# Four interleaved sequence layers on one core: a new order of all the work, and another last chunk

## The chip, the cores and the metric

The kernel runs on one core of one Trainium2 chip. A core has four engines that compute side by side, each with its own instruction queue: TensorE (PE, matrix products), VectorE (DVE), ScalarE (ACT) and GpSimd (POOL). SyncE (SP) issues nearly all DMAs here, in the order in which they stand in its queue. An engine takes its instructions in order: one that waits holds up all that stand behind it. The metric is the device time of one execution in microseconds (us).

## The reference

The input x has 2048 tokens of 640 channels, in bfloat16. Four layers are added to it one after the other, A, B, A, B, each behind a layer norm:

```python
x = A_x
x = x + A(layernorm(x)); x = x + B(layernorm(x), B_k, B_v, ...)
x = x + A(layernorm(x)); x = x + B(layernorm(x), B_k, B_v, ...)
```

Layer A is a diagonal state-space layer with 640 complex states. With `Lam_bar = exp(dt * Lam)` and `B_bar = ((Lam_bar - 1) / Lam) * B` it runs `h = Lam_bar * h + B_bar u_t` over the tokens and gives `2 Re(C h) + Dskip * u`.

Layer B multiplies its input by a long convolution: `k` is convolved with four taps per channel, multiplied by `v`, and the product is convolved along all 2048 tokens with the kernel `ssm_k` by FFT; `kv * ssm_D` is added. Call the result Y. Then `B(q) = q * Y`, with q the layer-normed x. Y does not depend on x, and both B layers use the same one. Both A layers have the same weights.

## The kernel before

**The work.** Y is computed first, in five passes of 128 channels (`y_pass`). A pass has FFT stages named KA, KB (of the kernel), VA, VB (of `k` times `v`), a product in frequency on DVE (pw, L1289 to L1294), and the way back (IB, a DMA transpose tt at L1326, IA, and the store to a scratch tensor `ysd` in DRAM at L1352). A stage is a handful of groups of matmuls, typically 16 of 128 columns (L1208, L1232 to L1237, L1313, L1342), each followed by the eviction of one PSUM tile, either on ACT (L384) or on DVE (L386). There are four PSUM tiles of 1024 columns. Beside the passes run the set-up of A's weights (`a_setup_tasks`: L543, L547, L563, L578, L599) and five blocks that make `k` times `v` (`kv_tasks`, L1163).

**Layer A** goes in four chunks of 512 tokens; a chunk has four quarters of 128 tokens. Per chunk:

- layer norm: statistics (in the first A by `bn_stats` at L698, later sums and squares on ACT at L668 and L673), the root on ACT (L678), its reciprocal on DVE (L683, L685), and its application (id: ACT L718 or DVE L720);
- a DMA transpose (tu, L748);
- the input projection (bp, L762 and L765) in groups of 40, 40 and 20 matmuls of 256 columns, each evicted by ACT at L384;
- three DVE products of 2560 columns (ri, L784 to L786), the carry (L795, L796), two scans (sc, L800, 1290 columns each), the carry for the next chunk (cy, L811 to L813), three more products (ro, L823 to L825);
- the output product in quarters (cp, L851: 30 or 25 matmuls in the second A), each evicted with the residual (xe: L863 on DVE, or ACT L859 in the first A).

Pairs of tokens share one scan step, so a chunk has 256 steps. The first A reloads its x (L1482) instead of keeping it. The scan of a chunk needs the carry of the chunk before, so the scans of one layer are a chain.

**Layer B** per chunk: load of Y from `ysd` (L1500), layer norm as above, its application (u, L718 or L720), one product with Y for the whole chunk (mm, L915, 2560 columns) and four additions (m, L921 in the first B; L923 in the second), and in the second B two stores of two quarters, 320 KB each (L886). In the second B's last chunk each quarter is a group of its own: statistics, u, a product of 640 columns (L915), an addition on DVE or POOL (L923), and a store of 160 KB (L881). Its last quarter takes another form: `(x + nmean) * Y` (L900), which needs only the mean, and then `rstd * that + x` (L904), which needs the root.

**What sets the order.** All of this is written as tasks: `S.add(name, engine, estimate, tasks before it, emit, uses=buffers)`. Before anything is emitted, `Sched.run` plays the tasks through once with their estimated durations. Whenever an engine is free, it takes the ready task of the highest rank, where the rank is minus the task's number in the table `WHEN`; a number is roughly the time at which a task should go, and it is a rank only, so a task never goes before those that it depends on. The order of the starts that come out is the order in which the instructions are emitted, so it is fixed on every engine. A task with two engines, such as `("act", "dve")`, takes the second when the first is busy for longer than the second number of its entry.

```python
t.rank, t.wait = (-when[0], when[1]) if isinstance(when, tuple) else (-when, 0.3)
...
cands = [t for t in ready if eng in t.engs and (t.engs[0] == eng or eng_free[t.engs[0]] > now + t.wait) and can(t)]
...
t = max(cands, key=lambda t: (t.rank, -t.idx))
```

Buffers also shape the order. The large SBUF tiles (13 of one size, 6 of double size) and the four PSUM tiles are handed out as tasks come up, and a task starts only when a tile is free for it.

Of the kernel before, what the change touches and what calls it, by code (L numbers as in the profile page):

```python
# [52 lines left out]
    "warm": -1.35, "yt_io0": 2.41, "yt_ph0": 8.42, "yt_sin0": 10.61, "yt_neg0": 12.73, "yt_io6": 10.07, "yt_ph6": 9.01, "yt_sin6": 12.27, "yt_neg6":  # L53
    15.91, "yt_io12": 13.05, "yt_ph12": 14.25, "yt_sin12": 15.9, "yt_neg12": 18.93, "yt_Ci": 20.28, "yt_Si": 37, "yt_nsi": 49, "yt_f0": 3.06, "yt_f2":
    4.09, "yt_f3": 7.55, "yt_f4": 6.22, "yt_h0": 0.91, "yt_h1": 0.33, "yt_h2": 5.52, "yt_h3": 5.63, "kv_dsl": 2.15, "kv_kd": 2.92, "kv_k0": 10.81,
    "kv_k1": 13.94, "kv_k2": 15.71, "kv_d0": 6.65, "kv_d1": 5.29, "kv_d2": 8.81, "kv_ds0": 11.35, "kv_lk0": 4.2, "kv_lv0": 5.45, "kv_mm0:0": 14.43,
    "kv_ev0:0": 16.51, "kv_mm0:1": 10.83, "kv_ev0:1": 13.08, "kv_st0": 17.9, "kv_ds1": 9.15, "kv_lk1": 12.7, "kv_lv1": 18.64, "kv_mm1:0": 19.27,
    "kv_ev1:0": 21.4, "kv_mm1:1": 21.75, "kv_ev1:1": 23.83, "kv_st1": 35.3, "kv_ds2": 18.43, "kv_lk2": 33, "kv_lv2": 29.5, "kv_mm2:0": 38.59, "kv_ev2:0":
    39.32, "kv_mm2:1": 43.65, "kv_ev2:1": 49.83, "kv_st2": 46.49, "kv_ds3": 43.37, "kv_lk3": 41.7, "kv_lv3": 45.49, "kv_mm3:0": 48.44, "kv_ev3:0": 50.96,
    "kv_mm3:1": 57.37, "kv_ev3:1": 61.07, "kv_st3": 92.99, "kv_ds4": 61.29, "kv_lk4": 49.28, "kv_lv4": 68.94, "kv_mm4:0": 73.9, "kv_ev4:0": 74.18,  # L60
    "kv_mm4:1": 69.76, "kv_ev4:1": 73.84, "kv_st4": 73.7, "a_pl": -0.06, "a_p0": 12.27, "a_p1": 16.9, "a_p2": 17.67, "a_p3": 18.1, "a_p4": 20.22, "a_p5":
    23.7, "a_p6": 27.16, "a_lamd": 27.66, "a_f": 28.77, "a_dd": 19.76, "a_ldB0": 1.15, "a_ldB1": -0.78, "a_wl00:0": 40.5, "a_wl00:1": 28.3, "a_wc00:0":
    44.32, "a_wm00:0": 48.24, "a_wc00:1": 49.59, "a_wm00:1": 52.87, "a_wl01:0": 44, "a_wl01:1": 31.8, "a_wc01:0": 48.88, "a_wm01:0": 52.09, "a_wc01:1":
    54.1, "a_wm01:1": 53.61, "a_wl02:0": 45.16, "a_wl02:1": 45.15, "a_wc02:0": 53.34, "a_wm02:0": 59.85, "a_wc02:1": 61.61, "a_wm02:1": 62.85, "a_wl03:0":
    70.24, "a_wl03:1": 64.21, "a_wc03:0": 77.95, "a_wm03:0": 76.93, "a_wc03:1": 78, "a_wm03:1": 78.68, "a_wl04:0": 66.45, "a_wl04:1": 65.36, "a_wc04:0":
    69.09, "a_wm04:0": 75.62, "a_wc04:1": 78.54, "a_wm04:1": 79.09, "a_b00:0": 10.52, "a_b0e0:0": 9.18, "a_b00:1": 8, "a_b0e0:1": (8.6, 99), "a_b00:2":
    13.66, "a_b0e0:2": (15.32, 0), "a_b00:3": 4.32, "a_b0e0:3": (8.39, 0.8), "a_b00:4": 17.45, "a_b0e0:4": (18.19, 0), "a_b01:0": 6.91, "a_b0e1:0": (7.2,
    0.8), "a_b01:1": 11.61, "a_b0e1:1": (14.74, 1.5), "a_b01:2": 4.71, "a_b0e1:2": (6, -1), "a_b01:3": 5.91, "a_b0e1:3": (6.61, 0), "a_b01:4": 8.47,
    "a_b0e1:4": (11.54, 1.5), "a_b10:0": 43.09, "a_b1e0:0": (45.04, 0.8), "a_b10:1": 40.99, "a_b1e0:1": (41.95, 3), "a_b10:2": 30.58, "a_b1e0:2": 31.69,
    "a_b10:3": 36.64, "a_b1e0:3": (39.19, 1.5), "a_b10:4": 47.48, "a_b1e0:4": (48.2, 3), "a_b11:0": 45.38, "a_b1e1:0": (46.36, 0.8), "a_b11:1": 32.76,  # L70
    "a_b1e1:1": (33.78, 6), "a_b11:2": 41.55, "a_b1e1:2": (40.73, -1), "a_b11:3": 31.52, "a_b1e1:3": 32.67, "a_b11:4": 29.62, "a_b1e1:4": (30.57, 0),
    "a_gm0": 80.21, "a_ge0": (84.11, 99), "a_gm1": 93.26, "a_ge1": 96.39, "a_gm2": 83.55, "a_ge2": (87.02, 6), "a_gm3": 89.92, "a_ge3": (93.2, 99),
    "a_gm4": 97.3, "a_ge4": (100.43, 0.8), "a_wl10:0": 85.18, "a_wl10:1": 91.79, "a_wc10:0": 95.59, "a_wm10:0": 101.44, "a_wc10:1": 122.34, "a_wm10:1":
    124.48, "a_wl11:0": 96.08, "a_wl11:1": 94.88, "a_wc11:0": 99.69, "a_wm11:0": 102.22, "a_wc11:1": 119.01, "a_wm11:1": 120.86, "a_wl12:0": 267.43,
    "a_wl12:1": 125.35, "a_wc12:0": 132.96, "a_wm12:0": 134.36, "a_wc12:1": 136.45, "a_wm12:1": 138.84, "a_wl13:0": 130.78, "a_wl13:1": 128.72,
    "a_wc13:0": 134.01, "a_wm13:0": 137.32, "a_wc13:1": 137.15, "a_wm13:1": 140.24, "a_wl14:0": 147.32, "a_wl14:1": 146.18, "a_wc14:0": 150.74,
    "a_wm14:0": 151.96, "a_wc14:1": 155.43, "a_wm14:1": 157.14, "a_ti": 21.54, "a_ta": 22.3, "a_t0": 24.96, "a_t1": 101.91, "a_t2": 108.08, "yq0_kl":
    8.92, "yq0_ka": 16.35, "yq0_KA:m0": 18.34, "yq0_KA:e0": (19.68, 1.5), "yq0_KA:m1": 21.46, "yq0_KA:e1": (22.64, 0.8), "yq0_KA:m2": 18.74, "yq0_KA:e2":
    (21.48, 6), "yq0_KA:m3": 19.03, "yq0_KA:e3": (20.58, 3), "yq0_KB:m0": 24.22, "yq0_KB:e0": (27.08, 99), "yq0_KB:m1": 24.89, "yq0_KB:e1": (26.18, 0),
    "yq0_KB:m2": 26.78, "yq0_KB:e2": 28.25, "yq0_KB:m3": 27.82, "yq0_KB:e3": (29.15, 6), "yq0_KB:m4": 23.99, "yq0_KB:e4": (27.98, 99), "yq0_vl": 20.98,  # L80
    "yq0_VA:m0": 31.28, "yq0_VA:e0": (31.91, 0.8), "yq0_VA:m1": 29.09, "yq0_VA:e1": (30.05, 3), "yq0_VA:m2": 32.18, "yq0_VA:e2": (32.81, 3), "yq0_VA:m3":
    29.37, "yq0_VA:e3": (30.95, 3), "yq0_VB:m0": 37.52, "yq0_VB:e0": (38.54, 0), "yq0_VB:m1": 34.93, "yq0_VB:e1": (36.27, 99), "yq0_VB:m2": 35.83,
    "yq0_VB:e2": (37.17, 1.5), "yq0_VB:m3": 34.04, "yq0_VB:e3": (35.37, 3), "yq0_VB:m4": 37.29, "yq0_VB:e4": (38.1, -1), "yq1_kl": 25.7, "yq1_ka": 32.42,
    "yq1_KA:m0": 38.31, "yq1_KA:e0": (39.88, -1), "yq1_KA:m1": 33.34, "yq1_KA:e1": (34.37, 6), "yq1_KA:m2": 40.32, "yq1_KA:e2": (40.95, 1.5), "yq1_KA:m3":
    33.62, "yq1_KA:e3": (34.34, -1), "yq1_KB:m0": 45.98, "yq1_KB:e0": (46.97, 0), "yq1_KB:m1": 55.1, "yq1_KB:e1": (56.01, 0), "yq1_KB:m2": 42.17,
    "yq1_KB:e2": (43.42, 0), "yq1_KB:m3": 50.15, "yq1_KB:e3": (51.4, 6), "yq1_KB:m4": 48.22, "yq1_KB:e4": (48.92, 0.8), "yq0_pw": 39.67, "yq0_IB:m0":
    54.21, "yq0_IB:e0": 55.94, "yq0_IB:m1": 52.95, "yq0_IB:e1": (54.57, 99), "yq0_IB:m2": 51.18, "yq0_IB:e2": (52.39, 99), "yq0_IB:m3": 52.09,
    "yq0_IB:e3": (53.31, -1), "yq0_IB:m4": 53.57, "yq0_IB:e4": (56.19, 99), "yq0_tt": 63.03, "yq1_vl": 49.03, "yq1_VA:m0": 54.86, "yq1_VA:e0": 56.03,
    "yq1_VA:m1": 53.39, "yq1_VA:e1": (53.81, 0), "yq1_VA:m2": 56.58, "yq1_VA:e2": (57.29, 0), "yq1_VA:m3": 56.61, "yq1_VA:e3": (51.46, 99), "yq1_VB:m0":
    60.95, "yq1_VB:e0": (65.88, 1.5), "yq1_VB:m1": 61.23, "yq1_VB:e1": (63.37, 0.8), "yq1_VB:m2": 62.8, "yq1_VB:e2": (66.49, 6), "yq1_VB:m3": 57.44,  # L90
    "yq1_VB:e3": (67.16, 0), "yq1_VB:m4": 62.47, "yq1_VB:e4": (62.27, 0), "yq0_IA:m0": 64.58, "yq0_IA:e0": (69.19, 0), "yq0_IA:m1": 66.1, "yq0_IA:e1":
    (67.34, 1.5), "yq0_st": 78.73, "yq2_kl": 48.68, "yq2_ka": 55.97, "yq2_KA:m0": 65.34, "yq2_KA:e0": (47.37, 6), "yq2_KA:m1": 66.58, "yq2_KA:e1": (67.98,
    0), "yq2_KA:m2": 66.35, "yq2_KA:e2": (71.01, 99), "yq2_KA:m3": 64.39, "yq2_KA:e3": (64.57, 0), "yq2_KB:m0": 79.33, "yq2_KB:e0": (81.23, 0),
    "yq2_KB:m1": 58.15, "yq2_KB:e1": (74.22, 0.8), "yq2_KB:m2": 71.59, "yq2_KB:e2": (78.27, 0.8), "yq2_KB:m3": 70.55, "yq2_KB:e3": (73.3, 99),
    "yq2_KB:m4": 77.69, "yq2_KB:e4": (78.01, 99), "yq1_pw": 66.29, "yq1_IB:m0": 73.36, "yq1_IB:e0": (75.43, 0), "yq1_IB:m1": 74.89, "yq1_IB:e1": (77.3,
    99), "yq1_IB:m2": 76.2, "yq1_IB:e2": (77.28, -1), "yq1_IB:m3": 76.99, "yq1_IB:e3": (78.62, 6), "yq1_IB:m4": 76.2, "yq1_IB:e4": (77.89, 1.5), "yq1_tt":
    86.38, "yq2_vl": 76.55, "yq2_VA:m0": 77.71, "yq2_VA:e0": (80.89, 0), "yq2_VA:m1": 79.71, "yq2_VA:e1": (81.79, 3), "yq2_VA:m2": 82.99, "yq2_VA:e2":
# [772 lines left out]
def b_chunk(S, nc, R, small, c, lname, s_x, sums_in, x_ready, s_Y, y_ready, sums_out, out, groups):  # L870
# [3 lines left out]
    def finish(q, t_m):  # L874
        ready.append(t_m)
        if out is None:
            return
# [11 lines left out]
    for qs in groups:  # L889
# [4 lines left out]
        for i, q in enumerate(qs):  # L894
# [11 lines left out]
            else:  # L906
# [6 lines left out]
                def e_mm(_, qs=qs):  # L913
                    b = s_b.get()[:, qs[0]:qs[-1] + 1, :]
                    nc.vector.tensor_tensor(b, b, s_Y.get()[:, qs[0]:qs[-1] + 1, :], ALU.mult)  # L915
# [627 lines left out]
```

## Time and profile before

| | us |
|---|---|
| median of 3 runs (lowest, highest) | 381.21 (380.71, 381.98) |
| the profiled execution itself | 381.21 |
| span of its profile | 379.5 |
| PE busy | 338.3 (89%) |
| DVE busy | 317.2 (84%) |
| ACT busy | 252.1 (66%) |
| POOL busy | 24.0 (6%) |

The span is what the engines' records cover; the 1.71 us between it and the execution's own time lie around it. Busy times are averages over stages with different limits: passes of FFT and set-up until about 140 us, then A and B chunks of the two halves, the last output quarters until 368.7, and what comes after the last matmul. So the profile has to be read by stretches, and a wait counts only where the engine that sets the pace is the one that waits. The granted TensorE clock (PEclk) is given as a share of full speed; its mean was 0.964. Where it is 0.5, a matmul takes twice its time while PE shows as busy. In rows of instructions, `b<-ps` means that a buffer is written from PSUM, `x16` counts instructions, and `<-DVE b L825` after a wait names what ended it.

### The profile page before, as it was taken

To read this page: it belongs to the slowest core of one execution; us is meant where nothing else is said; L and a number is where in the kernel's file an instruction comes from. 1 tells how busy PE (TensorE), PEld (TensorE's weight loads), DVE (VectorE), ACT (ScalarE), POOL (GpSimd) and SP (SyncE) were. 2 spreads that over 40 slices of the span, in tenths; PEclk is the share of its full clock that TensorE was granted. 3 is DMA by queue.
4 is the path that set the end of the run, shared out by engine and by line. 5 is a ranking of instruction groups with operands and counts; after the bars stand their busy time and mean duration, and the time that the engine had idled before them with its cause. 6 is when DMAs were issued, how large, how long until landed. Compare 5 with 4: busy or idle time off the path is not lost. (4 is left out here: it accounts for less than half of the span.)

```text
span 379.5 us, 8447 instructions
## 1 busy us (share of the span) xinstructions
PE 338.3 (89%) x3565; PEld 251.5 (66%) x3565; DVE 317.2 (84%) x474; ACT 252.1 (66%) x400; POOL 24.0 (6%) x54
## 2 busy tenths in 40 slices
PE   8787988889996899999999999979999999994780
PEld 8446867676685779989566766745867756852350
DVE  8689698886998888699999669914999899889586
ACT  2999878896899976864426577288592574910462
POOL 4650030000000000000000000000000000000022
PEclk9899999999998989999999999989999999998796
DMA  8979998899956993771752527005132003213003
GB/s 232 207 170 195 198 212 175 147 250 265 194 105 114 208 167 86 140 156 46 120 133 55 209 71 195 15 0 74 66 67 75 1 2 69 80 73 128 0 19 121
DMA packets 119000, 45.91 MB, mean 121 GB/s; under 512 B 111661, under 2 KB 113458, under 8 KB 118962
## 3 DMA queue, kind: packets, MB, share of 16 engines
q1 hardware_dynamic: 118816, 45.36, 55.3%
q8 instruction: 28, 0.46, 0.5%
q14 instruction: 10, 0.08, 0.1%
q10 hardware_dynamic: 146, 0.01, 0.0%
HBM read 17.38 MB, written 7.86 MB: 67 GB/s over the span
## 5 line engine op out<-in xcount | busy, mean ns | idle before, releaser
L384 ACT ACTIVATE b<-ps 128x1024 bf16<-128x1024 f32 (+3 forms) x121 | 106.2, 946 | 25.7 <-PE ps L765 18.8
L851 PEld LDWEIGHTS <-b 128*128 128x128 bf16 x880 | 68.5, 99 | 61.2 <-DVE b L825 8.0
L851 PE MATMUL ps<-W,b 128*128 128x128 bf16 (+1 forms) x640 | 99.4, 305 | 10.1 <-DVE b L825 7.7
L718 ACT ACTIVATE b<-b,nmr,rstd 128x640 bf16<-128x640 f32 (+1 forms) x46 | 39.7, 911 | 28.0 <-DVE nmr L685 26.6
L762 PE MATMUL ps<-b,BT 128*128 128x256 bf16 x400 | 57.3, 274 | 0.9 <-DMA b<-b 0.6
L765 PE MATMUL ps<-b,BT 128*128 128x256 bf16 x400 | 56.9, 273 | 0.0
L800 DVE TENSOR_TENSOR_SCAN b<-rtab,b 128x1290 bf16<-128x1290 f32 x16 | 44.7, 2832 | 0.2
L762 PEld LDWEIGHTS <-BT 128*128 128x128 bf16 x400 | 38.6, 98 | 5.7 <-issue 1.2
L765 PEld LDWEIGHTS <-BT 128*128 128x128 bf16 x400 | 39.3, 98 | 4.7
L673 ACT ACTIVATE junk<-b,nmean 128x640 bf16<-128x640 f32 x48 | 39.7, 827 | 1.4
L1232 PE MATMUL ps<-b,b 128*128 128x128 bf16 x170 | 35.9, 224 | 4.0 <-ACT b L384 3.9
L386 DVE CAST b<-ps 128x1024 bf16<-128x1024 f32 (+2 forms) x28 | 29.1, 1059 | 11.9 <-PE ps L1237 6.0
L1235 PE MATMUL ps<-b,b 128*128 128x128 bf16 x170 | 36.1, 223 | 0.0
L1237 PE MATMUL ps<-b,b 128*128 128x128 bf16 x150 | 33.6, 224 | 0.0
L1234 PE MATMUL ps<-b,b 128*128 128x128 bf16 x150 | 33.6, 224 | 0.0
L851 PE MATMUL ps<-G,b 128*128 128x512 bf16 (+1 forms) x160 | 27.0, 299 | 0.0
L668 ACT ACTIVATE nmean<-sums 128x4 f32<-128x4 f32 (+1 forms) x15 | 3.0, 202 | 35.5 <-DVE b L863 25.5
L1163 PE MATMUL ps<-b,fd 128*128 128x512 bf16 x80 | 20.3, 397 | 4.5 <-ACT b L384 1.6
L923 POOL TENSOR_TENSOR b<-b,b 128x640 bf16<-128x640 bf16 x3 | 4.8, 1638 | 306.1 <-DMA out_dram<-b 306.1
L859 ACT ACTIVATE b<-ps 128x640 f32<-128x640 f32 x15 | 10.4, 695 | 14.8 <-PE ps L851 14.8
L1313 PE MATMUL ps<-b,b 128*128 128x128 bf16 x160 | 19.1, 219 | 0.9 <-DVE b L386 0.6
L1208 PE MATMUL ps<-FA,b 64*128 64x128 bf16 x320 | 14.8, 223 | 5.1 <-ACT b L384 3.8
(203 smaller groups left out, 591.5 us busy)
## 6 DMA issues: line engine op xcount, KB each, us to landing
b<-in_A_x_dram SPq DMA_DIRECT2D x8, 640.0 KB, 4.6
b<-ysd SPq DMA_DIRECT2D x8, 640.0 KB, 4.2
b<-in_B_ssm_k_dram SPq DMA_DIRECT2D x5, 512.0 KB
kvd<-b SPq DMA_DIRECT2D x5, 512.0 KB, 5.0
b<-kvd SPq DMA_DIRECT2D x5, 512.0 KB, 4.7
ysd<-b SPq DMA_DIRECT2D x5, 512.0 KB, 5.0
out_dram<-b SPq DMA_DIRECT2D x6, 320.0 KB, 2.2
W<-in_A_B_im_dram SPq DMA_DIRECT2D x1, 800.0 KB, 4.9
```

The costliest lines, as they stand in the source:

```text
L384: nc.scalar.activation(out, in_, ACT.Copy)
L386: nc.vector.tensor_copy(out, in_)
L673: nc.scalar.activation(small.junk, src(q), ACT.Square, bias=st["nmean"][:, i:i + 1], scale=1.0, accum_out=st["ssq"][:, i:i + 1])
L718: nc.scalar.activation(dst, src, ACT.Identity, bias=st["nmr"][:, i:i + 1], scale=st["rstd"][:, i:i + 1])
L762: nc.tensor.matmul(pb[:, jj, c2, :], lhsT=aw["BT1"][:, c2, j, k, :], rhs=uT[:, 0:2, k, :], start=(k == 0), stop=False)
L765: nc.tensor.matmul(pb[:, jj, c2, :], lhsT=aw["BT0"][:, c2, k, j * P:(j + 1) * P], rhs=uT[:, 2:4, k, :], start=False, stop=(k == NJ - 1))
L800: nc.vector.tensor_tensor_scan(gv, rt, gv, 0.0, ALU.mult, ALU.add)
L851: nc.tensor.matmul(pc[:, o0:o1], lhsT=lh, rhs=rh, start=(n == 0), stop=(n == len(ops) - 1))
L1232: nc.tensor.matmul(ps[:, g, 0, :], lhsT=T["Cf"].get()[:, q, :], rhs=are, start=True, stop=single)
L1234: nc.tensor.matmul(ps[:, g, 0, :], lhsT=T["Sf"].get()[:, q, :], rhs=A[:, 2 * q + 1, :], start=False, stop=True)
L1235: nc.tensor.matmul(ps[:, g, 1, :], lhsT=T["NSf"].get()[:, q, :], rhs=are, start=True, stop=single)
L1237: nc.tensor.matmul(ps[:, g, 1, :], lhsT=T["Cf"].get()[:, q, :], rhs=A[:, 2 * q + 1, :], start=False, stop=True)
```

## The change

Three things are changed; the other code is the same, apart from line numbers, which move by 2 up to `finish` and by 10 behind it. A shorter computation of the factor f of A's weights (L495) and the place of the first layer's square roots behind the sine tables are in both versions alike.

1. The table `WHEN` is a new one: every one of its numbers is replaced, so the order of work changes on PE, DVE, ACT, POOL and SP, along with some choices of engine for evictions and for the application of the norm. Five entries are gone with the tasks that they belonged to. A few of them, before and after:

```diff
-    "A1c0_bp:0": 116.12, "A1c0_bp:1": 121.21, "A1c0_bp:2": 133.57, "A1c0_sc": 145.49,
+    "A1c0_bp:0": 123.4, "A1c0_bp:1": 129.1, "A1c0_bp:2": 139.11, "A1c0_sc": 149.24,
...
-    "A2c3_ri": 305.5, "A2c3_sc": 307.47, "A2c3_ro": 320.11, "B2c1_mm": 281.11, "B2c1_m:0": 285.53, "B2c2_mm": 332.68,
+    "A2c3_ri": 313.25, "A2c3_sc": 309.77, "A2c3_ro": 323.9, "B2c1_mm": 336.41, "B2c1_m:0": 377.53, "B2c2_mm": 352.56,
```

Around the last scan, DVE's queue had, in this order: ri of the last chunk of A, mm and four m of the second B's chunk 1, the carry, two scans, one xe, ro, three xe. It now has ri, the carry, two scans, two xe, ro, and mm and m of that chunk only after the next xe's.

2. In the last chunk of the second B, all four one-quarter groups take the form of L900 and L904, where only the last one did, and the additions L923 run on DVE alone.

3. The last chunk is stored in two stores of 320 KB instead of four of 160 KB.

```diff
     def finish(q, t_m):
         ready.append(t_m)
-        if out is None:
-            return
-        if len(groups) > 1:
-            def e_st(_):
-                r0 = c * TOK + (q >> 1) * 2 * P
-                nc.sync.dma_start(out=out[r0:r0 + 2 * P, :].rearrange("(i q) d -> i q d", q=2)[:, q & 1], in_=s_Y.get()[:, q, :])
-            S.add(f"{lname}c{c}_st:{q}", "sp", 0.4, ready[-1:], e_st, xt=0.5, uses=[s_Y])
-        elif q % 2 == 1:
+        if out is not None and q % 2 == 1:
             def e_st(_, t=q >> 1):
...
-            if qs[0] == 3:
+            if len(qs) == 1:
                 def e_u(_, q=q, i=i, bu=bu, st=st):
...
-                            (nc.gpsimd if eng == "pool" else nc.vector).tensor_tensor(s_Y.get()[:, q, :], b, x, ALU.add)
-                    engs, ests = (("dve", "pool"), (0.77, 1.4)) if out is not None and c >= NCH - 2 else ("dve", 0.83 if out is None else 0.77)
-                    t_m = S.add(f"{nm}_m:{q}", engs, ests, [t_mm], e_m, uses=[s_b, s_Y, s_x])
+                            nc.vector.tensor_tensor(s_Y.get()[:, q, :], b, x, ALU.add)
+                    t_m = S.add(f"{nm}_m:{q}", "dve", 0.83 if out is None else 0.77, [t_mm], e_m, uses=[s_b, s_Y, s_x])
```

The product mm, which is now made for whole chunks only, is written without its range of quarters.

## The prediction

> **What bounds the kernel now.** I read first the table by stretches, cut where the character of the trace changes: engines' busy time, the granted TensorE clock, DMA share.
>
> ```profile
> core 0: us, PE busy (x) PEld busy (x) DVE busy (x) ACT busy (x) POOL busy (x), PEclk, DMA share, GB/s
> 0.00:140.00 140.00, 120.36 (x1629) 94.57 (x1630) 117.42 (x211) 118.28 (x155) 19.12 (x51) 0.96 0.95 191
> 140.00:245.00 105.00, 104.33 (x1031) 80.18 (x1029) 90.80 (x107) 59.71 (x100) 0.00 (x0) 1.00 0.49 113
> 245.00:285.00 40.00, 37.03 (x297) 25.91 (x295) 27.39 (x41) 30.57 (x61) 0.00 (x0) 0.96 0.27 50
> 285.00:346.00 61.00, 60.99 (x504) 42.25 (x502) 56.67 (x76) 30.69 (x55) 0.00 (x0) 1.00 0.22 66
> 346.00:353.10 7.10, 0.07 (x1) 0.07 (x2) 7.07 (x7) 0.00 (x0) 0.00 (x0) 0.70 0.00 0
> 353.10:368.70 15.60, 15.54 (x110) 8.51 (x110) 10.14 (x26) 9.27 (x22) 1.07 (x1) 0.92 0.03 12
> 368.70:379.50 10.80, 0.00 (x0) 0.00 (x0) 7.74 (x12) 3.62 (x9) 3.76 (x3) 0.69 0.29 106
> ```
>
> PE is the bound: from 140 to 368.7 it is busy except for 0.7 us before 245, 3.0 in 245–285 and 7.0 at 346–353. The change leaves every matmul in place (3565 in the page), so it can win only PE's idle time, its slow clock, and the 10.8 us after the last matmul. In 0–140 PE idles 19.6 us, while DVE and ACT carry 117 and 118 of 140 and DMA 0.95. The end of that stretch in windows of 20 us, same columns:
>
> ```profile
> 100.00:120.00 20.00, 16.25 (x269) 13.16 (x268) 18.91 (x28) 19.72 (x26) 0.00 (x0) 1.00 0.57 101
> 120.00:140.00 20.00, 17.20 (x232) 15.14 (x232) 17.17 (x26) 17.57 (x23) 0.00 (x0) 0.83 1.01 209
> ```
>
> PE idles 6.5 us, and a clock of 0.83 over 20 us loses 3.4 more. Next the waits of PE over the whole span, and DVE's in 236–285: total us, times, longest.
>
> ```profile
> PE ps L851 <- DVE b L825: 7.7, 2, 7.0
> PE ps L1232 <- ACT b L384: 3.9, 7, 1.2
> PE ps L1208 <- ACT b L384: 3.8, 9, 1.1
> PE ps L851 <- ACT b L384: 2.4, 1, 2.4
> ```
> ```profile
> DVE rstd L683 <- ACT std L678: 10.8, 2, 6.4
> ```
>
> The 7.0 is the hole at 346; the 2.4 lies at 250.0–252.4; the two in the middle are the transforms (L1208, L1232) waiting for evictions. What the clock does after a stall, PE alone:
>
> ```profile
> 253.30:256.70 3.40, 3.40 (x10) 0.50 0.00 0
> ```
>
> Half speed for 3.4 us, 1.7 us lost, right after the 2.4 us stall. Last the chain, around the hole, and DVE against POOL in the tail:
>
> ```profile
> 336.00 1.37 issue
> 337.38 1.50 DVE b L915
> 338.87 0.02 issue
> 338.89 3.03 DVE b L923 x4
> ...
> 342.30 5.58 DVE b L800 x2
> 347.88 0.72 DVE b L863 x2
> ...
> 353.03 15.63 PE ps L851 x110
> ```
> ```profile
> 367.63 4.83 POOL L923 TENSOR_TENSOR b<-b,b 128x640 bf16<-128x640 bf16 x3 [306.06 <-DMA out_dram<-b]
> 369.43 3.72 DVE L923 TENSOR_TENSOR b<-b,b 128x640 bf16<-128x640 bf16 x2
> 375.72 0.83 DVE L923 TENSOR_TENSOR b<-b,b 128x640 bf16<-128x640 bf16 x1
> ```
>
> DVE works on a finished chunk of B (L915, then four L923, 4.5 us) before the last scan (L800) that PE waits for.
>
> **The change, part by part.** (Line numbers of before.) The shorter f and the square roots behind the sine stand in both files alike, so they cost nothing here. What differs is the order and the last chunk of B.
>
> (1) *End stage, hole at 346.* From the last input-projection matmul (332.2) to the last L825 (353.0) before needs 20.8 us; PE has four output quarters left for it, two of 30 matmuls at 4.08 us and two of 25 at 3.0: 14.1, and runs dry for 7.0. In the new order DVE goes from L784–786 to carry, scans, two L863 and L823–825 with no L915 and L923 between: 20.8 − 4.5 + about 1.1 for two whole L863 (0.82 + 0.08 each) in place of 0.72 = 17.4. PE has six quarters behind its last projection: 3 × 4.08 + 3 × 3.0 = 21.2. Margin 3.8, so the hole goes: −7.0. The rest of that table, 353.03–355.7 at half clock, loses 1.3: −1.3. The displaced L915 and L923 come after the last L825, where DVE has slack: 10.14 of 15.6 at 353–369, and PE alone needs 15.6. L825 is no longer what PE waits for; PE's own work is.
>
> (2) *Middle, 245–285.* DVE stands 10.8 us at L683 for ACT's L678, which stands behind squares and evictions; PE then waits 2.4 for one eviction (L384). The new order has each reciprocal where the root before it on ACT comes sooner, and the projections further from their evictions. Ends: 0 (another wait takes its place) and −4.6, the 3.0 idle and 40 × 0.04 = 1.6 of clock. I take −4.6: laying the trace's durations end to end along the new order (each instruction behind the one before it on its engine and behind what it reads), I find no PE wait after 155 us, and the nearest row is the stretch after it, 60.99 of 61. 140–245: −0.7, ends 0 and −0.7.
>
> (3) *Early stage, 0–140.* An FFT step is 16 matmuls at 56 ns, 0.9 us, for one eviction of 1.03 (ACT L384) or 1.22 us (DVE L386); a projection group is 40 matmuls, 4.4 us, for one eviction of 1.03. A stretch of FFT alone is therefore eviction-bound, as 100–120 shows (ACT 19.72 of 20). The new order puts the first projection behind 1541 matmuls instead of 1593 and mixes more of them in (58 projection matmuls among the first 1600, before 6); the first output quarter comes after 1993 instead of 2117, the first scan 13 rows earlier on DVE. Ends: 0, and −10.0, the 3.75 + 2.8 of idle and 3.4 of clock in 100–140; the 13 us of idle in 0–100 I leave, as DMA is at 0.93 to 1.12 there. Between the two I take −6.0: the idle mostly goes, but the same laying-out leaves two PE stalls near 102 and 108, of 1.6 and 2.7 us, and with each may come a half-clock stretch of 1.7, as after the 2.4 us stall at 250. SP goes through the same transposes and loads in another order; its issues of 0.4 to 5.3 us are two fewer, in the stores of the tail alone. Three more evictions of 640 columns run on ACT (0.71 each), inside these ends.
>
> (4) *Tail.* Before: 10.8. Each of the four last groups now takes the pair L900/L904 (0.87, 0.88), at a pitch of 0.80; three L915 of 640 (0.49) and the L720/L718 go, and no L923 runs on POOL. After the last matmul: 0.25 to the last L863, 0.75, four L900 and four L904 at 0.80 = 6.4, reciprocal pairs on the path 0.5, one 320 KB store landing in 2.1 (before 160 KB, 1.8), 1.15 from the landing to the end of the span as in before (378.35 to 379.5): 11.1. L904 newly waits for ACT's root; behind it on DVE stands only the next quarter's pair, and its own store. The first paired store leaves one L904, 0.8, later than a single one, and lands before the second. I take +0.2; ends −1.5 (two L900 done before the last quarter) and +2 (all roots late). Gain inside it, already counted: two L923 beside POOL took 3.72, alone 2 × 0.82, so 2.1 lost. The page "SBUF — State Buffer", section on who interferes with whom, says that a VectorE instruction with two SBUF inputs and a GpSimd one that reads SBUF exclude each other for a whole instruction: by that rule two blocked for 1.64 each would have lost 3.3, more than the row. The row stands.
>
> On the clock: "TensorE: Matmul & The Clock Gate", on oscillation, asks for no PE gap above about 3.4 us. By it only the hole at 346 would cost clock and term (2) would be 3.0. The row of 0.50 after a 2.4 us stall disagrees.
>
> **Sum.** 379.5 − 7.0 − 1.3 − 4.6 − 0.7 − 6.0 + 0.2 = 360.1 of span. The profiled execution took 381.21, 1.71 more than its span, and equals the median of the three. 360.1 + 1.71 = 361.8.
>
> **Rivals.**
> *Early stage gives nothing.* DMA at 0.95 of 0–140 and both evictors near 84% speak for it; DMA's 0.57 in 100–120 against. Then 361.8 + 6.0 = 367.8.
> *The hole stays.* If evictions or L863 waits eat the 3.8 us of margin and 7 more, PE dries again: up to 361.8 + 8.3 = 370.1. For it: PE and DVE hang on each other there; against: no other long DVE work stands in the new path.
> *The order only moves the stalls.* Every gain comes back as another wait: 381.2. Against: 30 us of idle and clock would have to be matched anew.
> *Slower, by the Y store.* All B layers need Y in DRAM. SP issues in order, and a transpose held by a late eviction (L1326 after L386: up to 9.8; L1352 after L384: up to 11.2) holds all behind it. The last Y store was issued at 204.24 and landed at 208.0; its reload takes 4.2, the first L915 came at 216.2, so each us after a landing at 212 moves all of the second half. To be slower than 381.2 by 1.1, the 19.4 + 1.1 must be lost: landing after 212 + 20.5 = 232, two of the longest holds on end and 3 more. The new order has fewer FFT steps ahead of it late, which speaks against.
>
> **How the numbers follow.** Forecast 0.76 (own range 357.5 to 366), early stage nothing 0.13, hole stays 0.04, no change 0.02, slower 0.05. Range: full −10.0 early gives 357.8, half a microsecond less in the tail 357.3; upward 367.8 and 0.7 for (1)'s neighbours, 368.5. Within 0.3% (1.1 us, about what a measurement of this kernel can tell): 0.02. Faster 0.76 + 0.13 + 0.04 = 0.93, slower 0.05.
>
> **What would show it.** (1): no PE wait for the last read-out above 1 us, PE continuous into its last matmul, clock 1.0. (2): PE over 39.5 of 40 in the same stage, the L683 waits under 3 us. (3): the first scan some 10 us earlier; wrong if PE still idles 19 us before it. (4): last matmul to end about 11, no POOL L923, eight of the L900/L904 kind. It is wrong as a whole if PE waits anywhere after the first scan for more than 3 us together.

## The result, and the profile after

The changed kernel takes 364.54 us (median of 4 runs, 363.01 to 366.37) against 381.6 for the kernel before (380.71 to 382.58): a ratio of 0.955, 95% interval 0.950 to 0.961, 17 us less. The profiled execution took 365.61 with a span of 363.8; it is 1.1 above the median, and the sums below are made against it, so against 379.5 of span before.

The table by stretches of the changed kernel, cut as before; the later cuts follow the shorter span:

```profile
core 0: us, PE busy (x) PEld busy (x) DVE busy (x) ACT busy (x) POOL busy (x), PEclk, DMA share, GB/s
0.00:140.00 140.00, 120.04 (x1630) 95.39 (x1631) 117.83 (x203) 115.69 (x155) 20.18 (x51) 0.98 0.97 184
140.00:245.00 105.00, 103.64 (x1057) 79.47 (x1054) 96.20 (x126) 75.05 (x132) 0.00 (x0) 1.00 0.50 121
245.00:285.00 40.00, 40.00 (x338) 28.85 (x336) 37.33 (x44) 22.46 (x42) 0.00 (x0) 1.00 0.29 66
285.00:334.00 49.00, 49.00 (x399) 33.80 (x397) 42.31 (x53) 23.76 (x43) 0.00 (x0) 1.00 0.18 42
334.00:352.50 18.50, 18.43 (x153) 10.99 (x150) 17.33 (x37) 12.82 (x30) 0.00 (x0) 1.00 0.22 72
352.50:363.80 11.30, 0.00 (x0) 0.00 (x0) 7.63 (x14) 1.42 (x4) 0.00 (x0) 0.63 0.30 116
```

From 154 us to its last matmul PE waits for nothing that the table of waits names. From 245 on it idles 0.1 us, where before it idled 3.0 and 7.0, and the clock is at full speed there, where before two half-clock stretches took 1.7 and 1.3. Together that is 12.9 of the 15.7 us of span. DVE is busy for 37.33 of 40 us in 245 to 285, where it was 27.39. The first 140 us look as before: PE busy for 120.04, before 120.36. The first scan starts at 154.1 instead of 163.0, but 1804 matmuls are done by then instead of 1903, so this is mostly another order of the same work. The rest of the gain, 15.7 − 12.9 = 2.8, is 3.3 won before 245 less 0.5 lost behind the last matmul.

The table of PE's waits over the whole span shows what is left in the early stage (an eviction, a load, an eviction), in us, times, longest. The lines are those of the changed kernel, where L384 of before is L382 and L851 is L849:

```profile
PE ps L1303 <- ACT b L382: 2.8, 2, 2.4
PE ps L1153 <- DMA b<-in_B_k_dram: 2.7, 1, 2.7
PE ps L1222 <- ACT b L382: 2.0, 3, 1.1
```

DVE behind the last matmul, in the timeline (start, us, line): the last L861, four L891 (the old L900) and four L895 (the old L904), none beside POOL.

```profile
352.46 0.82 DVE L861 SCALAR_TENSOR_TENSOR b<-ps,b 128x640 f32<-128x640 f32 x1
353.21 2.47 DVE L891 SCALAR_TENSOR_TENSOR b<-b,nmean,b 128x640 bf16<-128x640 f32 x3
...
358.52 1.67 DVE L895 SCALAR_TENSOR_TENSOR b<-b,rstd,b 128x640 bf16<-128x640 bf16 x2
```

### The profile page after: what moved, and what is told of

The parts are those of the page before. It is cut to its first block, busy times and chain, and to the rows that moved or that the text cites. A ratio compares the mean times of both kernels' runs of the same rounds, so it can differ in the third digit from the quotient of the medians.

```text
span 363.8 us, 8416 instructions
## 1 busy us (share of the span) xinstructions
PE 331.1 (91%) x3565; PEld 248.5 (68%) x3565; DVE 318.6 (88%) x473; ACT 251.2 (69%) x401; POOL 20.2 (6%) x51
## 4 chain that ended last, share of the span: by engine, by line
PE 68%; DMA 6%; ACT 6%; DVE 3%; issue 1%; DVEq 0%; ACTq 0%
PE ps L849 32%; PE ps L760 11%; PE ps L763 11%; PE ps L597 4%; ACT b L382 3%; PE ps L1153 2%; DMA b<-in_B_k_dram 2%; DMA b<-b 2%; PE ps L1303 2%; PE ps L1304 1%; DMA b<-in_A_x_dram 1%; DMA ysd<-b 1%; PE ps L1222 1%; PE ps L1198 1%; PE ps L1225 1%
## 5 line engine op out<-in xcount | busy, mean ns | idle before, releaser
L382 ACT ACTIVATE b<-ps 128x1024 bf16<-128x1024 f32 (+3 forms) x121 | 104.9, 924 | 31.3 <-PE ps L763 24.9
L849 PEld LDWEIGHTS <-b 128*128 128x128 bf16 x880 | 67.9, 98 | 48.3
L849 PE MATMUL ps<-W,b 128*128 128x128 bf16 (+1 forms) x640 | 96.0, 299 | 0.0
L760 PE MATMUL ps<-b,BT 128*128 128x256 bf16 x400 | 56.8, 273 | 1.4 <-DMA b<-b 1.4
L384 DVE CAST b<-ps 128x1024 bf16<-128x1024 f32 (+2 forms) x28 | 31.8, 1154 | 13.7 <-PE ps L1198 8.3
L760 PEld LDWEIGHTS <-BT 128*128 128x128 bf16 x400 | 38.4, 98 | 5.9 <-DMA b<-b 1.5
L716 ACT ACTIVATE b<-b,nmr,rstd 128x640 bf16<-128x640 f32 (+1 forms) x44 | 37.7, 916 | 5.2 <-DVE nmr L683 5.2
L1222 PE MATMUL ps<-b,b 128*128 128x128 bf16 x170 | 35.6, 222 | 2.7 <-ACT b L382 2.0
L1225 PE MATMUL ps<-b,b 128*128 128x128 bf16 x170 | 35.9, 222 | 0.0
L1224 PE MATMUL ps<-b,b 128*128 128x128 bf16 x150 | 33.3, 222 | 0.0
L1227 PE MATMUL ps<-b,b 128*128 128x128 bf16 x150 | 33.3, 222 | 0.0
L849 PE MATMUL ps<-G,b 128*128 128x512 bf16 (+1 forms) x160 | 27.0, 299 | 0.0
L1303 PE MATMUL ps<-b,b 128*128 128x128 bf16 x160 | 19.2, 219 | 2.8 <-ACT b L382 2.8
L545 DVE SCALAR_TENSOR_TENSOR W<-b,s_F 128x640 bf16<-128x640 bf16 x20 | 17.5, 883 | 2.7 <-ACT b L541 2.4
L1304 PE MATMUL ps<-b,b 128*128 128x128 bf16 x160 | 19.1, 219 | 0.0
L541 ACT ACTIVATE b<-b,s_F 128x640 f32<-128x640 bf16 x20 | 16.5, 836 | 3.7 <-DMA b<-in_A_C_im_dram 1.9
```

The lines of the kernel that those rows point to most:

```text
L382: nc.scalar.activation(out, in_, ACT.Copy)
L384: nc.vector.tensor_copy(out, in_)
L716: nc.scalar.activation(dst, src, ACT.Identity, bias=st["nmr"][:, i:i + 1], scale=st["rstd"][:, i:i + 1])
L760: nc.tensor.matmul(pb[:, jj, c2, :], lhsT=aw["BT1"][:, c2, j, k, :], rhs=uT[:, 0:2, k, :], start=(k == 0), stop=False)
L849: nc.tensor.matmul(pc[:, o0:o1], lhsT=lh, rhs=rh, start=(n == 0), stop=(n == len(ops) - 1))
L1222: nc.tensor.matmul(ps[:, g, 0, :], lhsT=T["Cf"].get()[:, q, :], rhs=are, start=True, stop=single)
```

## The experiments

Two readings of the 12.9 us stood against each other. The one of the prediction: the new late order does it directly, above all by taking 4.5 us of DVE work out of the path to the last read-out. The rival: something further up decides whether DVE has work in 205 to 285, and the hole at 346 is only where the lost DVE time shows. Each number of the table is a rank, so a kernel can take some of them from the one table and some from the other. Every row shows the lines of its own kernel, and the tables differ in length; for instance, L851 of before (the output product) is L863, L861 or L862 in these kernels, L825 (the last of the read-out products) is L837, L835 or L836, L915 (the product with Y) L927 or L918.

**1. The last chunk alone.** The code of the changed kernel, the whole table of before.

> The new last chunk of B (four pairs of L900/L904 form, two paired stores, nothing on POOL) with the table of before, so the order of before. Theory of the prediction, term (4) alone: +0.2, 381 to 382. Rival: the four pairs put more work on DVE alone behind the last matmul than the old forms, which shared it with ACT and POOL; then 1 to 3 us slower than before, 382.5 to 384.5. Either way the hole of 7 us before the last read-out stays.

381.78 us, beside 381.72 for the kernel before; ratio 1.000 (0.997 to 1.003). The new last chunk by itself neither costs nor saves anything that can be measured, and the hole of 7.0 us stays. All of the gain is in the table.

**2 and 3. The late numbers alone, and the early numbers alone.**

```diff
# late numbers (early numbers: the two tables exchanged)
-WHEN = new
+WHEN = {k: new[k] if k[:2] in ("B1", "A2", "B2") else old[k] for k in new}
```

> The changed kernel, but only the tasks of the second layer on (B1, A2, B2) take the new table's numbers; set-up, FFT passes and first A keep those of before. Theory of the prediction: terms (1) and (2) are in the late order, 13 us; so about 368 to 370, the hole at 346 and the stall at 250 gone. Rival, that the early order decides: first scan stays at 163, the last Y store at 204 to 208, and the later stages stay as starved as before; then 378 to 382 with 6 to 9 us of PE stalls after 245.

> The mirror image: set-up, FFT passes and first A take the new numbers, B1, A2 and B2 keep those of before. Theory of the prediction: term (3) alone, 3 to 6 us, so 375 to 378, with the hole at the end still there. Rival: the earlier first scan and the earlier Y store let the later stages run without starving; then within 2 us of the changed kernel, 363 to 367, first scan at 152 to 155, no PE stall above 1 us after 250.

Late numbers alone: 379.80, ratio 0.9965 (0.9937 to 0.9994), 1 to 2 us. Early numbers alone: 364.73, ratio 0.957 (0.953 to 0.961), all of the change. The same stretch of both, late numbers first, columns as above:

```profile
245.00:285.00 40.00, 37.44 (x305) 26.37 (x304) 31.61 (x45) 26.86 (x56) 0.00 (x0) 1.00 0.17 40
```
```profile
245.00:285.00 40.00, 40.00 (x337) 28.84 (x336) 37.42 (x44) 23.04 (x42) 0.00 (x0) 1.00 0.25 62
```

This is against the prediction's attribution. The kernel with the early numbers has the late numbers of before, and still no hole: its trace has the product L915 of the second B's chunk 1 at 337.6, behind the last scan at 322.2, where the kernel before had it at 337.4, ahead of the last scan at 342.3. The number of that task is 281 in both. The planner sends a task when its inputs and its engine are ready, so the late order is made by what comes before it more than by its own numbers.

**4. Only the work ahead of the last scan moved.** In the kernel before, five numbers.

```diff
-    "B2c1_mm": 281.11, "B2c1_m:0": 285.53, "B2c1_m:1": 304.2, "B2c1_m:2": 282.79, "B2c1_m:3": 283.18,
+    "B2c1_mm": 321.0, "B2c1_m:0": 321.1, "B2c1_m:1": 321.2, "B2c1_m:2": 321.3, "B2c1_m:3": 321.4,
```

> The kernel before, with one thing moved: the product L915 and the four additions of the second B's chunk 1 go behind the last read-out instead of in front of the last scan. Theory of the prediction, term (1) by itself: the hole shrinks from 7 to about 2.5 us and the time falls by as much or, with the clock, a little more: 375 to 377. Rival: DVE is short of time to the end, so the 4.5 us come back behind the last matmul: hole 2.5, last matmul some 4.5 us earlier, stretch behind it 4 to 6 us longer, 380 to 383.

384.36, ratio 1.008 (1.006 to 1.011): nothing is won. PE's wait for the last read-out, in the waits from 285 on, and the stretches around the last matmul:

```profile
PE ps L863 <- DVE b L837: 2.6, 1, 2.6
```
```profile
340.00:366.00 26.00, 22.04 (x177) 12.85 (x174) 21.26 (x35) 8.29 (x24) 0.00 (x0) 1.00 0.15 52
366.00:382.60 16.60, 0.00 (x0) 0.00 (x0) 12.71 (x14) 4.09 (x7) 6.97 (x4) 0.62 0.21 79
```

The hole shrank from 7.0 to 2.6, the last matmul starts at 364.4 instead of 368.4, and what was saved is lost behind it: 12.71 us of DVE work, where before it was 7.74 behind 368.7. The product of chunk 1 now took the place of that of chunk 2, and chunk 2's went behind the last matmul. DVE did idle for 4.7 of the 26 us in 340 to 366, 3.2 of them in one wait for PE's output matmuls: the time was there, but the next instruction of its queue was not ready for it.

Two things besides the move lengthen this run. Up to 337 us every engine's queue stands as in the kernel before, and yet the profiled execution is 1.8 us later at the first scan already (164.75 against 162.99). And behind the last matmul four additions on POOL, before three, held DVE's instructions up by 4.4 us, before by 2.1 (shown in the last section). So the run shows that the move wins nothing here, not that it costs 3 us; the same move with the new last chunk, which has no POOL additions, was not run.

**5. The base for further runs.** In this kernel and all that follow, the 45 transposing DMAs are plain copies of as many bytes; the data come untransposed, and times are compared within these kernels.

```diff
-nc.sync.dma_start_transpose(out=kT[:, KPAD:KPAD + L], in_=B_k[0][:, kb * P:(kb + 1) * P])
+nc.sync.dma_start(out=kT[:, KPAD:KPAD + L], in_=B_k[0].rearrange("(p a) d -> p (a d)", p=P)[:, kb * L:(kb + 1) * L])
...
```

> The kernel before, order unchanged, with all 45 transposing DMAs (k, v, C, the normed x, the FFT tables and the FFT's way back) made plain copies of as many bytes between the same buffers, so the data come untransposed and the output is not the reference's. It is the base that the next kernels are compared with. A 512 KB transpose took 5.7 to 6.1 us to land, a plain load of 512 KB 4.7 to 5.8. If the transposes' length holds PE up in the early stage: first scan earlier than 158 (163 in before), time 370 to 377. If not: first scan within 3 us of 163, 378 to 382. The hole before the last read-out stays at 5 us or more either way, as its order is the same.

> The changed kernel with the same 45 plain copies. Difference to the kernel before with plain copies: 14 to 18 us faster if the gain is one of order, under 10 if it lay mostly in how the transposes queued. If DMA is what PE's 20 us of idle in 0 to 140 come from: first scan below 149 and time 357 to 361; if evictions bound the early stage: first scan within 2 us of 154, time 361 to 365.

With plain copies the order of before takes 380.17 (ratio to the kernel before 0.997, 0.994 to 1.000), the new order 361.49 (0.945, 0.942 to 0.948): 18.7 us apart. So the gain is one of order, and not of how transposes queue. The first scan of the new order comes at 151.1 instead of 154.1, and the time falls by 3.0: the length of the transposes is worth that much in the new order and about 1 in the old. DMA's share of 0 to 140 fell from 0.97 to 0.65 for it, and PE was busy for 122.22 instead of 120.04.

**6. Two numbers.** The late numbers with plain copies, and the same with two of the early numbers set close to those of the new table (206.18 and 202.81), so that PE takes two output quarters of the first A's chunk 1 ahead of the first two projection groups of chunk 3:

```diff
-    "A1c3_bp:0": 168.83, "A1c3_bp:1": 168.45,
+    "A1c3_bp:0": 208.0, "A1c3_bp:1": 207.6,
```

> The kernel of the late numbers (B1, A2, B2 new, the rest as before) with plain copies. From the runs with transposes: 1 to 4 us faster than the kernel before with plain copies, DVE idle for 10 us or more in the 40 us after the first A's last scan, PE stalls of 5 to 9 us behind it.

> The same kernel of the late numbers with plain copies, and two further numbers: the first two projection groups of the first A's last chunk (A1c3_bp:0, :1) get 208 and 207.6 instead of 169 and 168, so PE takes the last two output quarters of chunk 1 ahead of them, and DVE has the first B's chunk 1 to work on before that chunk's scan. The early stage is as in the kernel of the late numbers. Theory that the head start of the early stage is itself what the later stages gain by: no change, within 2 us of the kernel of the late numbers. Rival, that the order in which DVE gets its work at 205 to 245 decides: 7 to 12 us faster than the kernel of the late numbers, no PE stall above 1 us behind the first A's last scan, DVE busy above 35 of the 40 us after 245.

380.43 without (0.997, 0.995 to 0.999), 368.13 with the two numbers (0.964, 0.960 to 0.968): 12.3 us, and the first scan is at 162 in both. The stretches 205 to 285 without and with:

```profile
205.00:245.00 40.00, 40.00 (x337) 28.68 (x335) 32.18 (x42) 21.53 (x43) 0.00 (x0) 1.00 0.32 110
245.00:285.00 40.00, 37.88 (x315) 26.67 (x312) 31.60 (x43) 27.41 (x58) 0.00 (x0) 1.00 0.15 50
```
```profile
205.00:245.00 40.00, 39.09 (x328) 27.84 (x326) 32.38 (x46) 28.94 (x63) 0.00 (x0) 1.00 0.30 110
245.00:285.00 40.00, 39.64 (x332) 28.28 (x331) 37.78 (x43) 21.90 (x43) 0.00 (x0) 1.00 0.19 66
```

What DVE waits for in 205 to 285, and PE from 200 on, first without, then with:

```profile
DVE rstd L693 <- ACT std L688: 11.9, 3, 5.0
DVE b L918 <- ACT b L728: 3.3, 3, 1.7
```
```profile
PE ps L772 <- DVE b L873: 3.2, 1, 3.2
PE ps L861 <- DVE b L835: 3.0, 1, 3.0
PE ps L861 <- ACT b L394: 1.9, 1, 1.9
PE ps L772 <- DMA b<-b: 0.9, 1, 0.9
```
```profile
DVE b L918 <- ACT b L728: 6.1, 3, 3.8
DVE rstd L693 <- ACT std L688: 1.6, 1, 1.6
```
```profile
PE ps L772 <- DMA b<-b: 0.9, 1, 0.9
PE ps L861 <- DVE b L835: 0.4, 1, 0.4
```

With the old place of the projection, DVE stands for a root three times, first until 223.9, and does chunk 3's products and scan (224.8 to 239.5) before the first B's product for chunk 1 (241.7). With the new place that product goes at 225.9, while chunk 3's scan is 7 us later (236.6 instead of 229.6); the second A's first scan is 6.7 us earlier all the same (260.6 instead of 267.3), and the last one 14 (326.2 instead of 340.3). The early stage is the same in both, so the head start isn't needed for this part. The planner works out all that follows anew, so the two kernels differ in more than those two groups from there on; what is shown is that the order from about 205 on, at equal early stages, is worth 12 us of the 18.7.

**7. The two numbers on the old table, and the product moved back in the new one.**

> The kernel before with plain copies and only the two numbers (A1c3_bp:0 and :1 to 208 and 207.6), all other numbers as before. If the place of these two projection groups is enough by itself: 8 to 12 us faster than the kernel before with plain copies, 368 to 372. If it needs the late numbers too, because DVE would then take the chunks of A and B in the old order all the same: within 3 us, 378 to 384.

386.34 (ratio 1.013, 1.010 to 1.017): 6 us slower than the old order with plain copies. With the old late numbers the same move makes PE run dry twice, for 8.0 us at 238 and 7.0 at 350:

```profile
PE ps L863 <- DVE b L837: 16.1, 4, 8.0
```

> The changed kernel with plain copies, and five numbers altered: the first B's product for chunk 1 and its four additions go behind the read-out of A's chunk 3 on DVE, as they stood in the kernel before. The head start of the early stage stays. If the place of that product alone decides: most of the 12 us that two numbers gave in the kernel of the late numbers are lost, 370 to 374. If DVE only has to be kept busy, with whatever work there is: the displaced 4.8 us come back later, and 2 to 6 us are lost, 363.5 to 367.5. If the head start covers all of it: no loss, 360 to 362.

In the new order the first B's product and additions for chunk 1 were given numbers of 232.0 to 232.4 instead of 215.5 to 223.4, so that they come behind chunk 3's read-out. 366.14, ratio 0.960 (0.956 to 0.964) beside 0.945: 4.7 us by the medians are lost, and a hole opens again in front of the last read-out (334.5 to 337.4):

```profile
PE ps L862 <- DVE b L836: 3.0, 1, 3.0
```

But the edit did not do what it was made for. The product stayed where it was (217.7, without the edit 217.8); two of its four additions went behind chunk 3's scan, and chunk 2's product came at 249.5 instead of 242.7. DVE was busy for 72.1 us of 205 to 285, without the edit for 72.4, so nothing was lost there. The loss lies in 285 to 334, without the edit first, then with it:

```profile
285.00:334.00 49.00, 49.00 (x402) 32.83 (x400) 42.07 (x53) 25.71 (x46) 0.00 (x0) 1.00 0.12 41
```
```profile
285.00:334.00 49.00, 48.84 (x397) 32.56 (x395) 38.57 (x51) 21.96 (x42) 0.00 (x0) 1.00 0.11 41
```

DVE waits there for evicted projections, twice, 8.0 us together (6.0 of it in one wait that ends at 321.9), where it waited 0.5; the last scans end 7.7 us later, at 332.3 instead of 324.6. So idle time of DVE ahead of the last scan goes with a stall of PE again, here 13 us later, and 205 to 285 is not the only place for it. How the edit led to the late projection is not shown.

**8. What holds PE up before 140.** In the new order with plain copies, less work for ACT, or less for DVE:

```diff
# less for ACT: scaling of C
-nc.scalar.activation(s_wr.get()[1], s_wr.get()[0][:, 1, :], ACT.Copy, scale=...)
+nc.scalar.activation(s_wr.get()[1][:, 0:8], s_wr.get()[0][:, 1, 0:8], ACT.Copy, scale=...)
...
# less for DVE: three of the six products in frequency
-nc.vector.tensor_tensor(t1, t1, t2, ALU.subtract)
+nc.vector.tensor_tensor(t1[:, 0, 0:8], t1[:, 0, 0:8], t2[:, 0, 0:8], ALU.subtract)
...
```

> The changed kernel with plain copies, and ACT's twenty scalings of C cut from 640 columns to 8, so W comes out wrong: about 14 us less ACT work before 150. If evictions queued behind other ACT work make PE's 20 us of idle there: first scan 3 to 8 us earlier than 151, time 354 to 359. If DVE or the chain of the passes makes it: first scan within 1.5 us of 151, 360 to 363.

> The changed kernel with plain copies, and three of the six products in frequency (pw) cut to 8 columns in each of the five passes, so Y comes out wrong: 15 x 1.25 = 19 us less DVE work, three quarters of it before 130. If DVE's load makes PE's idle time in the early stage: first scan 3 to 10 us earlier than 151, time 352 to 358. If not: first scan within 1.5 us of 151, 360 to 363.

360.82 (0.947, 0.943 to 0.951) and 359.80 (0.943, 0.939 to 0.947), beside 361.49 (0.945): 0.7 and 1.7 us, neither clear of its interval. The first 140 us with plain copies alone, with less ACT work, with less DVE work:

```profile
0.00:140.00 140.00, 122.22 (x1677) 98.84 (x1678) 119.58 (x205) 118.09 (x158) 20.18 (x51) 0.99 0.65 192
```
```profile
0.00:140.00 140.00, 122.16 (x1671) 97.87 (x1672) 119.16 (x205) 109.72 (x158) 20.17 (x51) 0.98 0.65 193
```
```profile
0.00:140.00 140.00, 124.60 (x1695) 100.40 (x1696) 107.58 (x207) 118.99 (x159) 18.98 (x51) 0.96 0.65 194
```

Eight us less of ACT work change nothing in PE's busy time, twelve less of DVE give 2.4. The clock blurs both: before 140 the first of these executions has one half-clock stretch of 3.4 us, the second two and the third three, each worth 1.7. The two executions with less DVE work whose mean clock (0.984, 0.986) was that of plain copies alone (0.985 to 0.986) took 358.15 and 359.14, 2.3 to 3.3 below 361.49. So DVE's load is worth some 2 to 3 us there, and none of the three (DMA, ACT, DVE) bounds the stage by itself: PE's idle time of 15 to 20 us is made of many short waits on several engines. What bounds it is open.

## Why the prediction was right, and where it was wrong

The forecast was 361.8, the time is 364.54, inside the range. By its own steps, on the profiled executions (predicted span −19.4, measured −15.7):

- **(1), the hole: the sum was right.** It has two sides: the path, which is the time from the end of the last projection matmul to the end of the last read-out product on DVE; and the output matmuls that PE has left for that time, all but the last chunk's, which need that read-out. Before, there were 110 of them (four quarters), which took 14.1 us; in the changed kernel there are 165 (six quarters), which took 21.2. The path less the time of these matmuls gives the hole in the twelve kernels below (read from their timelines):

  | kernel | path, us | output matmuls | hole, us |
  |---|---|---|---|
  | before; new last chunk alone; before with plain copies | 21.1 in each | 110 | 7.0 in each |
  | two numbers on the old table | 21.0 | 110 | 7.0 |
  | product behind the last scan (experiment 4) | 16.6 | 110 | 2.6 |
  | late numbers; the same with plain copies | 17.1; 17.1 | 110 | 3.0; 3.0 |
  | product moved back (experiment 7) | 17.1 | 110 | 3.0 |
  | early numbers | 16.9 | 160 | 0 |
  | late numbers with the two numbers | 17.4 | 165 | 0 |
  | changed; the same with plain copies | 17.4; 17.4 | 165 | 0; 0 |

  So the product in DVE's way made 4 to 4.5 of the 7.0 us, and the rest went only where two more quarters stood behind the last projection. The prediction counted both.
- **(1) and (2), what was wrong: where it comes from and what it is worth by itself.** Predicted −7.0 − 1.3 − 4.6 = −12.9, measured −12.9: no idle time behind 245, PE at 40.00 of 40, and the waits at the reciprocal (L681) are 2.2 us in all. But the prediction read the new order off as if its late part could be had by itself, and the displaced work as free: "come after the last L825, where DVE has slack". Experiment 4 moved that work and nothing else, and nothing was won. The late numbers took the product out of the way, but left 110 matmuls; PE still idled 8.9 us between 245 and its last matmul, before 10.0, only in other places, and the time was 379.80. The two further quarters came with the early numbers, or with two numbers at 205 (experiment 6): there the last projection ends at 320.3 instead of 333.9, with 165 output matmuls left instead of 110.
- **Why the last projection comes earlier** is argued and not shown. It fits DVE's idle time in 205 to 285: 20.5 us before, 16.2 with the late numbers and plain copies, 9.8 with the two numbers, 7.3 in the changed kernel. Before, DVE lost 12.6 us in 245 to 285 and then had 63.7 of 68 us to do from 285 to 353, so it could not catch up; PE met that loss 60 to 100 us later, as a hole. In experiment 7 the idle time lay in 285 to 334 (10.4 us, without the edit 6.9). No run gave DVE idle time and changed nothing else. The prediction named DVE's standing at L683 and priced it by PE's own idle time beside it, 3.0 (the 2.4 of it lie at 250.6 to 252.9, not at 250.0 to 252.4); it did not connect it with the 7.0.
- **140 to 245.** Predicted −0.7, measured +0.7: one wait of 1.4 for a transposed x at the input projection (L760).
- **(3), mis-sized.** Predicted −6.0, measured −4.0 (−3.3 before 245, of which +0.7 are those of the point above). The step that failed is "the idle time mostly goes". It did not go, it moved: 120 to 140 is full (PE 19.89 of 20, before 17.20), as the mixing of projections was to do, but 60 to 80 has 15.69 instead of 17.58, with 2.7 us of waiting for a load of k, and 100 to 120 has 14.34 instead of 16.25. By the prediction's own sign (PE still idle for 19 us before the first scan) the term is wrong: PE idled 21.3 us ahead of it, before 19.6. What was won came otherwise: by 245 PE had made 476 projection matmuls instead of 451, in 1.0 us less of busy time. One half-clock stretch less (two, before three) accounts for 1.7 us of that; where the rest comes from is not shown. The two stalls foreseen near 102 and 108, of 1.6 and 2.7 us, came at 106.6 and 111.9, with 1.1 and 2.4.
- **(4), nearly right.** Predicted 11.0 to 11.1 behind the last matmul, measured 11.3; the last chunk alone is worth nothing (experiment 1).
- **The rivals.** The late Y store did not come: its last issue is at 194.84, where before it was at 204.24. The early stage gave about two thirds of the forecast, between the forecast and its rival of 367.8. That the hole stays holds in part for experiment 4 (2.6 us of it) and for the late numbers alone (3.0). With these alone the rival "the order only moves the stalls" came nearly true as well.

## What to carry to other kernels

A stall of the bounding engine has two sides: the other engine's way to the point that it waits for, and the work that the bounding engine has in hand until then. Count both. Here their difference gave the hole to 0.1 us in twelve kernels, and what PE had in hand was decided by the order from 205 on, 140 us ahead of the hole. A stall that shrinks is not yet time won: with 4.5 us of work taken out of the way the hole fell by 4.4 us, and the kernel was no faster. In a list-scheduled kernel a rank has no price of its own, since two numbers were worth 12 us in one table and cost 6 in another. A sum can be right for the whole change while no part of the change can be had at its price; only runs that change one half at a time tell.

## What the runs showed of the hardware

An exclusive wait between DVE and POOL showed down to the smallest instruction. In experiment 4, behind the last matmul, with an addition on POOL running:

```profile
372.60 5.53 POOL L935 TENSOR_TENSOR b<-b,b 128x640 bf16<-128x640 bf16 x3 [2.16 <-DVE b L927]
372.85 2.02 DVE L935 TENSOR_TENSOR b<-b,b 128x640 bf16<-128x640 bf16 x1
374.79 0.15 DVE L695 RECIPROCAL rstd<-std 128x1 f32<-128x1 f32 x1
374.97 1.17 DVE L697 TENSOR_TENSOR nmr<-nmean,rstd 128x1 f32<-128x1 f32 x1
```

The product of one element per partition (L697), which takes 0.16 alone, took 1.17; the reciprocal beside it (L695), with one input, took its usual 0.15. The additions L935 on DVE took 1.91 and 2.02 instead of 0.82, and L916 behind them 2.02 instead of 0.88. The waiting goes both ways: one addition, at 376.06, took its usual 0.81, and the POOL addition that began beside it 2.05, where the first one took 1.44. This agrees with the Trainium skill's "SBUF — State Buffer", section on who interferes with whom: two SBUF inputs contend with POOL, one does not.

A DMA share of 0.97 over 140 us bounded little: at 0.65, with the same bytes, the new order was only 3.0 us faster.

The clock fell to half for 3.4 us in 75.6 to 79.0 of the changed kernel, from 2 us into the wait of 2.7 for k (73.6 to 76.3), and since its first matmul PE had not been idle for 3.4 us anywhere. The stall of 2.4 that ends at 114.3 was followed by half speed at 120 in the changed kernel, and by none with plain copies, where it ends at 112.3. The stall of 2.4 at 250 of the kernel before, with half speed behind it, came at 252 in experiment 4, and the clock stayed at 1.00 there. Which stalls cost clock is not settled by these runs.
